# Gates of five chunks of an mLSTM scan on 80 partitions at once, with the first loads and row writes in another order

## The chip, the cores and the metric

The kernel runs on one core of one Trainium2 chip. The metric is the device time of one execution in microseconds (us), median of several runs. Smaller is better. In the views below PE is TensorE's matmul, PEld its weight load, DVE is VectorE, ACT is ScalarE, POOL is GpSimd, SP is SyncE, and SPq is SyncE's queue of DMA issues.

## The reference

Three layers run one after the other. The first is a gated linear attention (mLSTM) over 768 steps for 2 batches of 8 heads of 40 columns; its output, as 1536 tokens of 320 columns, goes through a routed mixture of experts (8 experts, 192 tokens each) and then through a dense mixture of 4 experts. The change touches only the first layer:

```python
for t in range(S):
    m_new = np.maximum(f_gate[:, :, t] + m, i_gate[:, :, t])
    f_stab = np.exp(f_gate[:, :, t] + m - m_new)
    i_stab = np.exp(i_gate[:, :, t] - m_new)
    m = m_new
    C = f_stab[:, :, None, None] * C + i_stab[:, :, None, None] * np.einsum('bhd,bhe->bhde', vt, kt)
    n = f_stab[:, :, None] * n + i_stab[:, :, None] * kt
    h_tilde = np.einsum('bhde,bhe->bhd', C, qt)
    nq = np.einsum('bhd,bhd->bh', n, qt)[:, :, None]
    denom = np.maximum(np.abs(nq), 1.0)
    y[:, :, t] = o * h_tilde / denom
```

## The kernel before

**Chunks and units.** The 768 steps are cut into six chunks of 128 steps. A unit is one chunk of one batch (8 heads); the loop runs over twelve units, `(c, b)` in the order (0,0), (0,1), (1,0) and so on. Inside a unit the recurrence is a masked matrix product: `scores` (L318) multiplies keys by queries, `spread` (L294 on TensorE, L301 on ScalarE) builds the matrix of decays, `weigh` (L326) multiplies the two on VectorE, `inner` (L349) multiplies the result by the values. Across chunks a state `C` is carried: `query` (L343) reads it, `outer` (L355) makes its increment from values that `weigh_v` (L309) has weighted, and `epilogue` (L358 to L406) adds both parts, normalises, and writes the token tile `xr` to `x_dram` (L405), to which a small load of `domain_probs` (L401) must have added four columns. `turn` and `logit` (L411, L420) then transpose that tile and compute its routing logits. TensorE's order within the loop's pass n is: scores of unit n+1, query and inner and outer of unit n, spread of the next unit or two, logit of unit n-2, turn of unit n-1. A spread needs both PSUM banks `db0` and `db1` (one buffer each) back from ScalarE. In pass 3 two spreads stand one behind the other, and ScalarE then opens the output gates with a sigmoid, which needs a change of its table before and after.

**Gates.** `gate(c0, c1)` computes on VectorE, for chunks c0 to c1, on 16 partitions (one for each batch and head): the running maximum `mm` by a scan along the steps (L242), the log decays (L244, L245), their running sum within the chunk `cum` (L257), a rounded copy `dhi`, and three more rows of `g3`. It is called three times: for chunk 0, chunk 1, and chunks 2 to 5, the last in two pieces around the weigh of unit (0,1). `gate_t` turns `g3` by TensorE and ScalarE into `gtr`, in which a step is a partition, and `decays` makes `dec`, the decay of a whole chunk. `rows(c)` copies the 16 rows of `dhi` for chunk c into partition 0 of one of two buffers, `MR[c % 2]`, by a DMA on SyncE's queue. The spread of chunk c reads that buffer.

**Queues.** Nearly every load is issued by SyncE in the order of the code, one behind the other: output gates (640 KB), queries and keys `qk` (416 KB for one batch of chunk 0, 832 KB for a whole chunk), keys and values `kv` (648 KB a chunk). The order is written by hand; no scheduler changes it.

## Time and profile before

| what | value |
|---|---|
| time, median of 3 runs | 651.18 us (650.54 to 651.72) |
| profiled execution, its own time | 650.6 us |
| its span, first to last instruction | 648.9 us |
| first 100 us (the scan): busy PE, DVE, ACT | 90.33, 71.70, 62.75 us |
| mean granted TensorE clock: 0 to 100, 100 to 137, after 137 us | 0.86, 0.58, 0.99 |

The scan takes about the first 100 us. The clock is told as a share of 2.4 GHz: 1.00 is the upper level and 0.50 the lower one of 1.2 GHz. A long row in a timeline may be the same work at the lower level.

### The profile page before, as it was taken

How to read it: one execution, taken by the hardware profiler on the slowest of the kernel's cores; microseconds unless marked ns; L12 is line 12 of the kernel's file. 1: busy time of each engine (PE TensorE's matmuls, PEld its weight loads, DVE VectorE, ACT ScalarE, POOL GpSimd, SP SyncE). 2: the span in 40 equal slices, each digit the busy share in tenths (PEclk: the TensorE clock that was granted, in tenths of full speed). 3: DMA queues.
4: the chain of work that ended last, by engine and by line, in shares of the span. 5: the costliest groups of instructions: out<-in, count | busy, mean ns of one | idle time of the engine just before them, and what ended most of it. 6: DMA issues, size and time to landing. Idle time of an engine off the chain costs nothing.

```text
span 648.9 us, 11110 instructions
## 1 busy us (share of the span) xinstructions
PE 604.2 (93%) x4411; PEld 529.5 (82%) x4416; DVE 296.8 (46%) x1116; ACT 182.0 (28%) x486; POOL 80.2 (12%) x126
## 2 busy tenths in 40 slices
PE   7989994588999999899999999999999999999996
PEld 3879992277887778797898989898989898989885
DVE  8744887877787666303242232322234231313221
ACT  8648720012222225422221113221123211111120
POOL 6000000201220124300110001200011000002022
PEclk9867997569999999999999999999999999999998
DMA  6744415334534355901220002210000000001011
GB/s 186 233 127 120 121 51 191 105 126 147 188 105 153 118 188 203 338 11 34 66 82 0 1 1 65 67 48 0 1 2 1 0 1 1 0 1 41 0 41 41
DMA packets 13238, 52.01 MB, mean 80 GB/s; under 512 B 3499, under 2 KB 5131, under 8 KB 10491
## 3 DMA queue, kind: packets, MB, share of 16 engines
q1 hardware_dynamic: 9107, 25.10, 13.0%
q0 software_dynamic: 3904, 26.12, 11.5%
q8 instruction: 34, 0.56, 0.4%
q14 instruction: 17, 0.14, 0.1%
q10 hardware_dynamic: 176, 0.09, 0.1%
HBM read 46.91 MB, written 4.35 MB: 79 GB/s over the span
## 4 chain that ended last, share of the span: by engine, by line
PE 77%; DVE 10%; issue 6%; DMA 3%; POOL 2%; ACT 1%; POOLq 0%; SPq 0%; DVEq 0%
PE y L1187 8%; PE y L1189 8%; PE y L1188 8%; PE z L1175 7%; PE z L1177 6%; PE z L1176 6%; PE y L929 5%; PE px L349 4%; PE z L916 4%; PE z L1179 3%; PE z L1180 3%; PE pr L645 3%; PE st L318 2%; DVE cmp L598 2%; PE px L343 1%
## 5 line engine op out<-in xcount | busy, mean ns | idle before, releaser
L1227 DVE SCALAR_TENSOR_TENSOR h2l<-z,h2h 128x512 fp32r<-128x512 f32 x96 | 66.4, 692 | 240.5 <-ACT h2h L1226 239.4
L1226 ACT ACTIVATE h2h<-z 128x512 fp32r<-128x512 f32 x96 | 57.4, 598 | 263.9 <-PE z L1180 259.6
L1189 PE MATMUL y<-wh,h2l 128*128 128x320 f32 x384 | 118.6, 309 | 0.0
L1187 PE MATMUL y<-wh,h2h 128*128 128x320 f32 x384 | 118.4, 308 | 0.0
L1188 PE MATMUL y<-wl,h2h 128*128 128x320 f32 x384 | 118.1, 308 | 0.0
L1175 PE MATMUL z<-X2h,wh 128*128 128x512 f32 x192 | 76.7, 399 | 0.8 <-DVE X2l L964 0.8
L1187 PEld LDWEIGHTS y<-wh,h2h 128*128 128x128 f32 x384 | 72.1, 188 | 4.5
L1177 PE MATMUL z<-X2h,wl 128*128 128x512 f32 x192 | 75.7, 394 | 0.0
L1176 PE MATMUL z<-X2l,wh 128*128 128x512 f32 x192 | 75.3, 392 | 0.0
L1188 PEld LDWEIGHTS y<-wl,h2h 128*128 128x128 f32 x384 | 72.1, 188 | 4.0
L1189 PEld LDWEIGHTS y<-wh,h2l 128*128 128x128 f32 x384 | 72.0, 188 | 0.0
L929 PE MATMUL y<-h,w 128*128 128x192 f32 x256 | 55.7, 338 | 0.0
L916 PE MATMUL z<-xt,w 128*128 128x192 f32 x256 | 55.6, 338 | 0.0
L569 POOL TENSOR_TENSOR wl<-raw,wh 128x512 fp32r<-128x512 f32 x16 | 20.6, 1288 | 204.1 <-ACT wh L562 204.1
L916 PEld LDWEIGHTS z<-xt,w 128*128 128x128 f32 x256 | 42.0, 192 | 4.2 <-issue 3.8
L1177 PEld LDWEIGHTS z<-X2h,wl 128*128 128x128 f32 x192 | 36.0, 188 | 9.4
L929 PEld LDWEIGHTS y<-h,w 128*128 128x128 f32 x256 | 41.5, 190 | 2.6 <-issue 1.5
L645 PEld LDWEIGHTS <-oh 128*128 128x128 bf16 x504 | 21.0, 98 | 25.4 <-issue 15.5
L1175 PEld LDWEIGHTS z<-X2h,wh 128*128 128x128 f32 x192 | 36.0, 188 | 5.5 <-DVE X2l L964 1.1
L919 ACT ACTIVATE h<-z 128x192 f32<-128x192 f32 x64 | 21.2, 331 | 66.3 <-PE z L916 62.4
L1176 PEld LDWEIGHTS z<-X2l,wh 128*128 128x128 f32 x192 | 36.0, 188 | 4.5
L1179 PE MATMUL z<-X2h,wh 128*128 128x512 f32 x96 | 38.3, 399 | 0.0
(241 smaller groups left out, 860.1 us busy)
## 6 DMA issues: line engine op xcount, KB each, us to landing
raw<-in_m2w_dram SPq DMA_DIRECT2D x20, 512.0 KB, 3.7
qk<-in_qk_dram SPq DMA_DIRECT2D x5, 832.0 KB
kv<-in_kv_dram SPq DMA_DIRECT2D x6, 648.0 KB, 11.4
x_dram<-xr SPq DMA_DIRECT2D x12, 194.0 KB, 2.0
sig<-in_og_dram SPq DMA_DIRECT2D x1, 1280.0 KB
raw<-in_m2w_dram SPq DMA_DIRECT2D x4, 256.0 KB, 7.2
qk<-in_qk_dram SPq DMA_DIRECT2D x2, 416.0 KB
sig<-in_og_dram SPq DMA_DIRECT2D x1, 640.0 KB
```

The source lines that it names most:

```text
L645: T.matmul(pc[:, :NC], oh[:, c], cmp[:, c], start=(c == 0), stop=(c == NT - 1))
L916: T.matmul(Z[f], w1[:, k * F + f * P:k * F + (f + 1) * P], xt[:, k], start=False, stop=(k == 1), skip_group_check=True)
L929: T.matmul(Y[0][:, i * CAP:(i + 1) * CAP], w2[:, f * DM + i * P:f * DM + (i + 1) * P], h, start=(f == 0 and i == 0), stop=(f == NF - 1), s ...
L1175: T.matmul(z, hi[:, c], xh[:, k], start=(k == 0), stop=False)
L1176: T.matmul(z, hi[:, c], xl[:, k], start=False, stop=False)
L1177: T.matmul(z, lo[:, c], xh[:, k], start=False, stop=False)
L1179: T.matmul(z, hi[:, c], xh[:, 2], start=False, stop=False)
L1187: T.matmul(y[:, :DM], hh[:, ts], hi[:, c], start=(f == 0), stop=False)
L1188: T.matmul(y[:, :DM], hh[:, ts], lo[:, d], start=False, stop=False)
L1189: T.matmul(y[:, :DM], hl[:, ts], hi[:, c], start=False, stop=(f == NF - 1))
L1226: A.activation(hh, z, AF.Relu)
L1227: V.scalar_tensor_tensor(hl, z, 0.0, hh.bitcast(F32), op0=OP.max, op1=OP.subtract)
```

## The change

Chunk 0 is computed as before, on 16 partitions, with one edit in the order. Then one scan over 640 steps gives the running maximum of chunks 1 to 5. Two DMAs (`spread_max`) copy that maximum, once shifted by a step, from 16 partitions of 640 to 80 partitions of 128 (`mx`), where a partition is one chunk of one head. The raw gates come to the same 80 partitions as a second copy of the input (`fx` and `ix`, 40 KB each, loaded on ScalarE's queue at the start). `gates_rest` does the remaining eight operations once for 80 partitions, and one multiplication for the chunk decays in place of four. `gates_rest_t` transposes four blocks of 80 columns, and ScalarE evicts them in three instructions.

The order changes with it. The second batch of chunk 0 (`load(0, 1)`) is loaded ahead of `kv` of chunk 0; `qk` of chunk 1 is loaded ahead of the decay rows of chunk 1; the decay rows of chunks 1 and 2 are written one behind the other ahead of `kv` of chunk 1, and those of chunks 3, 4 and 5 in passes 1, 3 and 4 in place of 2, 4 and 5. The gates' transposes stand in pass 0 in place of before the loop and pass 1. In the diff, lines that are only taken out of `gate`, `gate_t` and `decays` are not repeated.

```diff
+            X = NCH - 1
+            XB = X * BH
+            g3 = big.tile([112, P], F32, name="g3")
+            dl, io, cum = (big.tile([BH, P], F32, name=n) for n in ("dl", "io", "cum"))
+            dhi = big.tile([BH, P], F32R, name="dhi")
+            fx, ix, dlx, cumx, rst = (big.tile([XB, P], F32, name=n) for n in ("fx", "ix", "dlx", "cumx", "rst"))
+            dhx = big.tile([XB, P], F32R, name="dhx")
+            mx = big.tile([XB, 2, P], F32, name="mx")
+            g4 = big.tile([XB, 3, P], F32, name="g4")
+            for t, r0 in ((fx, 0), (ix, BH)):
+                nc.scalar.dma_start(t, gatex[r0 // BH])
             pat = big.tile([P, P], F32, name="pat")
             step = big.tile([P, P], F32R, name="step")
             MR = [big.tile([P, BH, P], F32R, name=f"mr{i}") for i in range(2)]
-            sel = [big.tile([BH, P], F32, name=f"sel{r}") for r in range(2)]
-            own = [big.tile([BH, 2 * HB], F32, name=f"own{r}") for r in range(2)]
-            de = [big.tile([BH, NCH, 2 * HB], F32, name=f"de{r}") for r in range(2)]
+            sel = [big.tile([XB, P], F32, name=f"sel{r}") for r in range(2)]
+            own = big.tile([XB, X, BH], F32, name="own")
+            de = big.tile([XB, X, B, 2, HB], F32, name="de")
             dec = big.tile([P, NCH, 2 * HB], F32, name="dec")
             gtr = big.tile([P, 4, NCH, BH], F32, name="gtr")
             G.affine_select(MR[1], zero[:, :, None].to_broadcast([P, BH, P]), pattern=[[0, BH], [1, P]],
                             compare_op=OP.not_equal, fill=-BIG, base=1, channel_multiplier=-1)
             A.activation(own2, own2, AF.Sigmoid)
-            V.memset(rst.rearrange("p (c t) -> p c t", t=P)[:, :, 0:1], 0.0)
             V.memset(g3, 0.0)
+            G.affine_select(own, zero[:XB, :, None].to_broadcast([XB, X, BH]), pattern=[[-1, X], [-X, BH]],
+                            compare_op=OP.not_equal, fill=1.0, base=0, channel_multiplier=1)
...
-                nc.sync.dma_start(MR[c % 2][0:1].bitcast(F32), dhi[:, c * P:(c + 1) * P].bitcast(F32))
+                src = dhx.rearrange("(h c) t -> c h t", c=X)[c - 1] if c else dhi
+                nc.sync.dma_start(MR[c % 2][0:1].bitcast(F32), src.bitcast(F32))
+
+            ft, it = gt[0:BH], gt[32:32 + BH]
+
+            def scan_max(c0, c1):
                 s = slice(c0 * P, c1 * P)
+                V.tensor_tensor_scan(mm[:, c0 * P + 1:c1 * P + 1], ft[:, s], it[:, s], mm[:, c0 * P:c0 * P + 1],
+                                     op0=OP.add, op1=OP.max)
+
+            def gate(f, i, m0, m1, dl, cum, dhi, io, g, ge, gl, n):
+                V.tensor_add(dl, f, m0)
+                V.tensor_sub(dl, dl, m1)
+                if n == BH:
                     V.memset(dl[:, 0:1], 0.0)
+                V.tensor_tensor_scan(cum, rst[:n], dl, 0.0, op0=OP.mult, op1=OP.add)
+                V.tensor_scalar(dhi, cum, 0.0, None, op0=OP.add)
+                V.tensor_sub(io, i, m1)
+                V.tensor_sub(g, io, cum)
+                V.tensor_scalar(ge, g, cum[:, P - 1:P], None, op0=OP.add)
+                V.tensor_sub(gl, dhi.bitcast(F32), cum)
+
+            def gates_first():
+                p = bank("lg", bufs=2)
+                T.transpose(p[:, :112], g3, ident[:112, :112])
+                for k, f in enumerate((AF.Copy, AF.Exp, AF.Exp, AF.Exp)):
+                    A.activation(gtr[:, k, 0], p[:, 32 * k:32 * k + BH], f)
+
+            def spread_max():
+                for i in range(2):
+                    nc.sync.dma_start(mx[:, i], mm[:, P + i:S + i])
+
+            def gates_rest():
+                gate(fx, ix, mx[:, 0], mx[:, 1], dlx, cumx, dhx, dlx, g4[:, 0], g4[:, 1], g4[:, 2], XB)
+                V.tensor_scalar(de.rearrange("p c b r j -> p c (b r j)"), own, cumx[:, P - 1:P], None, op0=OP.mult)
+
+            def gates_rest_t():
+                p = bank("lg", bufs=2)
+                for k, x in enumerate((g4[:, 0], g4[:, 1], dhx.bitcast(F32), g4[:, 2])):
+                    T.transpose(p[:, XB * k:XB * k + XB], x, ident[:XB, :XB])
+                d = p[:, 4 * XB:4 * XB + 8 * X]
                 for r in range(2):
+                    T.matmul(d, sel[r], de[:, :, :, r], start=(r == 0), stop=(r == 1))
+                q = p[:, :4 * XB].rearrange("p (k h c) -> p k c h", k=4, h=BH)
+                A.activation(gtr[:, 0, 1:], q[:, 0], AF.Copy)
+                A.activation(gtr[:, 1:, 1:], q[:, 1:], AF.Exp)
+                A.activation(dec[:, 1:], d.rearrange("p (c h) -> p c h", h=8), AF.Exp)
 
...
-            for f in gate(0, 1):
-                f()
+            scan_max(0, 1)
+            gate(ft[:, :P], it[:, :P], mm[:, :P], mm[:, 1:P + 1], dl, cum, dhi, io, g3[0:BH], g3[32:32 + BH],
+                 g3[96:96 + BH], BH)
+            V.tensor_scalar(g3[64:64 + BH], dhi.bitcast(F32), 0.0, None, op0=OP.add)
+            rows(0)
+            load(0, 1)
             load_kv(0)
+            scan_max(1, NCH)
+            spread_max()
+            load(1)
             A.activation(own2, own2, AF.Exp)
-            gate_t(0, 1)
+            gates_first()
             spread(*units[0])
             scores(*units[0])
             warm(CR['W1'])
-            weigh_v(*units[0])
-            for f in gate(1, 2):
-                f()
-            load(0, 1)
-            load(1)
-            load_kv(1)
             V.memset(ohs[0][:, 0:1], 0.0)
             weigh(*units[0])
-            gates = gate(2, NCH)
-            for f in gates[:5]:
-                f()
             spread(*units[1])
+            weigh_v(*units[0])
+            gates_rest()
+            rows(1)
+            rows(2)
+            load_kv(1)
             nc.scalar.dma_start(wg, wgate)
             load_o(CR['SO'], NCH)
-            gate_t(1, 2)
-            decays(1, 2)
             for n, (c, b) in enumerate(units):
                 if b == 0:
                     if c + 2 < NCH:
                     query(c, b)
                 if n < last:
                     weigh(*units[n + 1])
-                if n == 0:
-                    for f in gates[5:]:
-                        f()
                 if n < 2:
                     warm(CR['W3'][n])
                 inner(c, b)
                     outer(c, b)
                 if n < last:
                     weigh_v(*units[n + 1])
-                if n == 1:
-                    gate_t(2, NCH)
-                    decays(2, NCH)
-                if n == 2:
-                    rows(3)
-                if n == 4:
-                    rows(4)
-                if n == 5:
-                    rows(5)
+                if n == 0:
+                    gates_rest_t()
                 while len(GG) < min(last + 1, n + 3 + (n >= 3)):
                     spread(*units[len(GG)])
-                if n == 1:
-                    rows(2)
+                if n in (1, 3, 4):
+                    rows({1: 3, 3: 4, 4: 5}[n])
...
+    gatex = gates.reshape(2, BH, NCH, P)[:, :, 1:].reshape(2, (NCH - 1) * BH, P)
```

SyncE's queue, from the decay rows of chunk 0 on. `mr_138` and `mr_139` are the two buffers of decay rows before, `mr_147` and `mr_148` the same two after the change; `xr` and `x_dram` belong to the first unit's epilogue. Before:

```order
L229 DMA mr_138<-dhi 1x16x128
L184 DMA kv<-in_kv_dram 128x1296
L229 DMA mr_139<-dhi 1x16x128
L180 DMA qk<-in_qk_dram 104x1024
L180 DMA qk<-in_qk_dram 104x2048
L184 DMA kv<-in_kv_dram 128x1296
L187 DMA sig<-in_og_dram 128x2560
L180 DMA qk<-in_qk_dram 104x2048
L184 DMA kv<-in_kv_dram 128x1296
L401 DMA xr<-in_dprob_dram 128x4
L405 DMA x_dram<-xr 128x388
L229 DMA mr_138<-dhi 1x16x128
```

With the change:

```order
L231 DMA mr_147<-dhi 1x16x128
L180 DMA qk<-in_qk_dram 104x1024
L184 DMA kv<-in_kv_dram 128x1296
L260 DMA mx<-mm 80x1x128 x2
L180 DMA qk<-in_qk_dram 104x2048
L231 DMA mr_148<-dhx 1x16x128
L231 DMA mr_147<-dhx 1x16x128
L184 DMA kv<-in_kv_dram 128x1296
L187 DMA sig<-in_og_dram 128x2560
L180 DMA qk<-in_qk_dram 104x2048
L184 DMA kv<-in_kv_dram 128x1296
```

The decay rows of chunk 2, the last row of the first list, have moved from behind the first write of `x_dram` to a place ahead of `kv` of chunk 1. The two copies of the maximum stand between `kv` of chunk 0 and `qk` of chunk 1.

VectorE, around the weigh (`pm`) of the first two units. Before, from the weigh of unit (0,0) on:

```order
L326 TENSOR_TENSOR pm_268<-st0_226,gg_217 128x512
L326 TENSOR_TENSOR pm_268<-st1_227,gg_217 128x512
L242 SCALAR_TENSOR_TENSOR mm_119<-gt_66,mm_119 16x512
L244 TENSOR_TENSOR dl_131<-gt_66,mm_119 16x512
L245 TENSOR_TENSOR dl_131<-dl_131,mm_119 16x512
L257 SCALAR_TENSOR_TENSOR cum_133<-rst_134,dl_131 16x512
L250 TENSOR_SCALAR dhi_135<-cum_133 16x512
L326 TENSOR_TENSOR pm_315<-st0_305,gg_280 128x512
L326 TENSOR_TENSOR pm_315<-st1_306,gg_280 128x512
L255 TENSOR_SCALAR g3_130<-dhi_135 16x512
L259 TENSOR_TENSOR io_132<-gt_66,mm_119 16x512
```

With the change, from the weigh of unit (0,0) to that of unit (0,1):

```order
L316 TENSOR_TENSOR pm_250<-st0_235,gg_226 128x512
L316 TENSOR_TENSOR pm_250<-st1_236,gg_226 128x512
L241 TENSOR_TENSOR dlx_137<-fx_135,mx_141 80x128
L242 TENSOR_TENSOR dlx_137<-dlx_137,mx_141 80x128
L245 SCALAR_TENSOR_TENSOR cumx_138<-rst_139,dlx_137 80x128
L246 TENSOR_SCALAR dhx_140<-cumx_138 80x128
L247 TENSOR_TENSOR dlx_137<-ix_136,mx_141 80x128
L248 TENSOR_TENSOR g4_142<-dlx_137,cumx_138 80x128
L249 TENSOR_SCALAR g4_142<-g4_142,cumx_138 80x128
L250 TENSOR_TENSOR g4_142<-dhx_140,cumx_138 80x128
L264 TENSOR_SCALAR de_152<-own_151,cumx_138 80x80
L316 TENSOR_TENSOR pm_304<-st0_294,gg_257 128x512
```

The gates of chunk 1, which stood ahead of the first of these rows, and those of chunks 2 to 5 are now one block of nine between the two weighs, and that block reads `mx`.

TensorE, from the outer product to the spread (`db`). Before, in pass 1:

```order
L355 MATMUL py_168<-wv_344,kv_204 40x41 x8
L276 MATMUL lg_449<-ident_69,g3_130 128x112 x4
L285 MATMUL lg_458<-de0_144,sel0_140 128x32
L285 MATMUL lg_458<-de1_145,sel1_141 128x32
L294 MATMUL db0_462<-mr1_139,step_137 128x512
L294 MATMUL db1_464<-mr1_139,step_137 128x512
```

With the change, in pass 0:

```order
L345 MATMUL py_171<-wv_266,kv_208 40x41 x8
L269 MATMUL lg_335<-ident_69,g4_142 128x80 x2
L269 MATMUL lg_335<-ident_69,dhx_140 128x80
L269 MATMUL lg_335<-ident_69,g4_142 128x80
L272 MATMUL lg_335<-de_152,sel0_149 128x40
L272 MATMUL lg_335<-de_152,sel1_150 128x40
L284 MATMUL db0_345<-mr1_148,step_146 128x512
L284 MATMUL db1_347<-mr1_148,step_146 128x512
```

The transposes of the gates and the products for the chunk decays have moved one pass earlier, ahead of the spread of unit (1,0).

## Rows read from the trace of the kernel before

**Rows 1.** The page's first line: the span of the profiled execution.
```profile
span 648.9 us, 11110 instructions
```

**Rows 2.** Stretches: us, busy PE, PEld, DVE, ACT, POOL (instructions), clock, DMA share, GB/s.
```profile
0.00:10.00 10.00, 8.28 (x34) 3.48 (x35) 8.11 (x31) 7.76 (x16) 6.11 (x31) 1.00 0.61 180
10.00:15.00 5.00, 2.27 (x12) 1.39 (x12) 4.79 (x12) 4.80 (x24) 3.85 (x3) 0.89 0.73 181
15.00:20.00 5.00, 4.78 (x29) 4.41 (x30) 4.69 (x7) 2.00 (x12) 0.78 (x5) 0.50 1.02 269
20.00:30.00 10.00, 9.95 (x120) 8.64 (x121) 8.27 (x25) 7.48 (x33) 0.00 (x0) 0.97 0.84 264
35.00:44.00 9.00, 9.00 (x62) 8.51 (x62) 1.63 (x5) 4.18 (x17) 0.00 (x0) 0.50 0.74 192
44.00:48.00 4.00, 2.46 (x24) 1.59 (x24) 3.13 (x12) 2.87 (x12) 0.00 (x0) 0.93 0.16 50
48.00:58.00 10.00, 10.00 (x74) 9.34 (x73) 2.85 (x9) 8.56 (x19) 0.00 (x0) 0.50 0.34 84
```

**Rows 3.** Pieces of the chain that ended last: start us, length us, what.
```profile
9.91 4.66 DMA qk<-in_qk_dram
...
31.81 2.11 DMA mr<-dhi
...
35.01 1.17 PE lg L420 x6
...
44.66 0.44 PE db L294
...
45.13 2.19 ACT gg L301 x8
...
47.86 0.94 PE lg L420 x6
...
57.28 1.12 PE db L294 x2
...
70.14 0.61 PE lg L420 x6
...
75.35 0.66 PE db L294 x2
```

**Rows 4.** TensorE's timeline: start us, length us, line, tiles, count, idle before.
```profile
8.06 0.70 PE L294 MATMUL db<-mr,step 128*128 128x512 f32 x2 [0.23 <-DMA mr<-dhi]
...
14.71 2.08 PE L318 MATMUL st<-qk 40*128 40x128 f32 x16 [2.71 <-DMA qk<-in_qk_dram]
...
21.29 0.73 PE L294 MATMUL db<-mr,step 128*128 128x512 f32 x2
...
25.73 0.60 PE L276 MATMUL lg<-ident,g 112*128 112x112 f32 x4
...
26.82 0.73 PE L294 MATMUL db<-mr,step 128*128 128x512 f32 x2
```

**Rows 5.** VectorE's timeline, from the gates of the second chunk on.
```profile
7.49 0.47 DVE L242 TENSOR_TENSOR_SCAN mm<-gt,mm 16x128 f32<-16x128 f32 x1
7.99 0.28 DVE L244 TENSOR_TENSOR dl<-gt,mm 16x128 f32<-16x128 f32 x1
...
8.62 0.41 DVE L257 TENSOR_TENSOR_SCAN cum<-rst,dl 16x128 f32<-16x128 f32 x1
9.07 0.21 DVE L250 TENSOR_SCALAR dhi<-cum 16x128 fp32r<-16x128 f32 x1
...
12.26 1.27 DVE L242 TENSOR_TENSOR_SCAN mm<-gt,mm 16x512 f32<-16x512 f32 x1
```

**Rows 6.** SyncE's queue: issues around the first write of a token tile.
```profile
13.04 1.10 SPq L401 DMA_DIRECT2D xr<-in_dprob_dram  x1
31.38 0.33 SPq L405 DMA_DIRECT2D x_dram<-xr  x1
```

**Rows 7.** ScalarE's timeline: the eight weighted values of one unit.
```profile
15.09 1.91 ACT L309 ACTIVATE wv<-kv,gtr 128x41 f32<-128x41 f32 x8
```

More of the change, by code (lines that the diff above doesn't have):

```diff
@@ L46, in tile_mlstm_moe_moe @@
 @with_exitstack
-def tile_mlstm_moe_moe(ctx: ExitStack, tc: tile.TileContext, gates, qk, kv, og, wgate, dprob,
+def tile_mlstm_moe_moe(ctx: ExitStack, tc: tile.TileContext, gates, gatex, qk, kv, og, wgate, dprob,
                        m1w1, m1w2, m2w, out, dbg=None):
@@ L193, in attention @@
             load(0, 0)
-            g3 = big.tile([112, S], F32, name="g3")
-            dl = big.tile([BH, S], F32, name="dl")
-            io = big.tile([BH, S], F32, name="io")
-            cum = big.tile([BH, S], F32, name="cum")
-            rst = big.tile([BH, S], F32, name="rst")
-            dhi = big.tile([BH, S], F32R, name="dhi")
+            X = NCH - 1
[9 more added lines that the diff above has]
+                nc.scalar.dma_start(t, gatex[r0 // BH])
             pat = big.tile([P, P], F32, name="pat")
@@ L211, in attention @@
             V.memset(rst, 1.0)
-            V.memset(rst.rearrange("p (c t) -> p c t", t=P)[:, :, 0:1], 0.0)
             V.memset(g3, 0.0)
+            G.affine_select(own, zero[:XB, :, None].to_broadcast([XB, X, BH]), pattern=[[-1, X], [-X, BH]],
+                            compare_op=OP.not_equal, fill=1.0, base=0, channel_multiplier=1)
             for r in range(2):
-                G.memset(own[r], 1.0)
-                for s_, b_ in ((1, 0), (-1, 0)):
-                    G.affine_select(own[r].rearrange("p (b j) -> p b j", j=HB), own[r].rearrange("p (b j) -> p b j", j=HB),
-                                    pattern=[[-H * s_, B], [-s_, HB]], compare_op=OP.is_ge, fill=0.0,
-                                    base=b_ - HB * r * s_, channel_multiplier=s_)
                 G.memset(sel[r], 0.0)
@@ L270, in gate_t @@
-            def gate_t(c0, c1):
-                n = c1 - c0
-                for i0 in range(0, n, 4):
-                    m = min(4, n - i0)
-                    p = bank("lg", bufs=2)
-                    for i in range(m):
-                        T.transpose(p[:, 112 * i:112 * i + 112], g3[:, (c0 + i0 + i) * P:(c0 + i0 + i + 1) * P],
-                                    ident[:112, :112])
-                    p3 = p[:, :112 * m].rearrange("p (i h) -> p i h", h=112)
-                    for k, f in enumerate((AF.Copy, AF.Exp, AF.Exp, AF.Exp)):
-                        A.activation(gtr[:, k, c0 + i0:c0 + i0 + m], p3[:, :, 32 * k:32 * k + BH], f)
@@ L282, in decays @@
-            def decays(c0, c1):
-                p = bank("lg", bufs=2)[:, :8 * (c1 - c0)]
-                for r in range(2):
-                    T.matmul(p, sel[r], de[r][:, c0:c1], start=(r == 0), stop=(r == 1))
-                A.activation(dec[:, c0:c1], p.rearrange("p (c h) -> p c h", h=8), AF.Exp)
+                V.tensor_tensor_scan(mm[:, c0 * P + 1:c1 * P + 1], ft[:, s], it[:, s], mm[:, c0 * P:c0 * P + 1],
[4 more added lines that the diff above has]
+                if n == BH:
+                    V.memset(dl[:, 0:1], 0.0)
+                V.tensor_tensor_scan(cum, rst[:n], dl, 0.0, op0=OP.mult, op1=OP.add)
[4 more added lines that the diff above has]
+                V.tensor_sub(gl, dhi.bitcast(F32), cum)
@@ L1284, in _layout @@
     m1w1 = np.concatenate([a1[:, :P], a1[:, P:2 * P], third], -1).reshape(E1 * P, -1)
-    arrays = dict(gates=gates, qk=qk, kv=kv, og=og, wgate=wg, dprob=dp, m1w1=m1w1, m1w2=w2(inputs["moe_w2"]), m2w=m2w)
+    gatex = gates.reshape(2, BH, NCH, P)[:, :, 1:].reshape(2, (NCH - 1) * BH, P)
+    arrays = dict(gates=gates, gatex=gatex, qk=qk, kv=kv, og=og, wgate=wg, dprob=dp, m1w1=m1w1, m1w2=w2(inputs["moe_w2"]), m2w=m2w)
     return {n: np.ascontiguousarray(a) for n, a in arrays.items()}
```

31 lines of the change are left out of this document (removed).

## Prediction, written before the changed kernel ran

> **What bounds the kernel now.** I read the page first, then the windows, the chain of work that ended last, and the timelines of the engines of the first 100 us. The profiled execution took 650.6 us, 1.7 more than its span [rows 1]; the median of the runs shown is 651.2, so 0.6 is added to what the trace gives. The change ends with the scan, so the scan's end is what counts: everything behind it waits for its logits, and I take it to move with them.
>
> The scan has one regular pace. From the logits of one pass to the spread of that pass the chain goes through TensorE alone, and a pass takes 75.35 - 70.14 = 5.21 us plus 0.66 for the spread, 5.87 in all [rows 3]. The first 58 us miss that pace in five places.
> - TensorE waits 2.71 us for `qk` of the second batch [rows 4], a load issued at 9.91 that lands 4.66 us later [rows 3].
> - It then works from 15 to 20 us at a clock of 0.50 [rows 2].
> - At 31.81 it waits 2.11 us for the decay rows of chunk 2 [rows 3]. Their issue stands in SyncE's queue behind the first `x_dram` write, which goes out only at 31.38 because the small `xr` load issued at 13.04 lies behind 4 MB of loads [rows 6].
> - After that wait the clock is 0.50 from 35 to 44 us [rows 2]: logits to end of spread, 35.01 to 44.66, take 9.65 us in place of 5.21 [rows 3].
> - In pass 3 the second spread waits for ScalarE (2.19 us in the chain at 45.13). TensorE is busy for 2.46 of the 4 us around it, and from 48 to 58 us the clock is 0.50 again [rows 2]: 47.86 to 57.28 take 9.42 us [rows 3].
>
> So each pause of some 1.5 to 2.7 us costs its length and then about four more.
>
> **The change, part by part.** *VectorE's work.* The call for chunk 1 and that for chunks 2 to 5 take 12 operations each, of 0.2 to 0.5 us and of 0.4 to 1.3 us [rows 5]. In their place stand one scan over 640 steps, estimated from 0.47 us at 128 and 1.27 at 512 [rows 5] as 1.54, and nine operations on 80 x 128. No row shows 80 partitions; the nearest are the same operations on 16 x 128. VectorE's duration might grow with the rows (five times as long, 14 us for the nine) or not at all (2.7 us with gaps); the weigh in the same place has 128 partitions and the page gives no sign of such growth, so I take 2.7. The saving itself is worth nothing: TensorE waits for loads while these operations run.
>
> *The maximum's round trip* is a new wait. The scan of chunk 1 began at 7.49 [rows 5]; with two memsets cut from 768 to 128 columns ahead of it I take 6.9 for the long one, which then ends near 8.4. The two `mx` copies are issued at 8.4 to 9.4. The least they can take is what a small row copy takes on an empty queue, 2.11 us [rows 3], so 10.5. But by the shapes 2.43 MB of loads stand up to and with them: gates 96 KB, `fx` and `ix` 80, output gates 640, `qk` twice 416, `kv` 648, `mx` 80. At 180 GB/s to 10 us and 181 from there [rows 2] these are through at 13.5. The trace's 4.66 us for 416 KB behind a `kv` load speaks for the late end, which I take: 13.5 (10.5 to 15).
>
> VectorE stands still from the first weigh (done at 11.8) to 13.5, with weigh (0,1) queued behind. TensorE needs that weigh only for the inner product of pass 1, at about 20, so the wait is covered by 3 us; beyond that it goes on the path. `dhx` is the fourth operation: 0.28 + 0.28 + 0.41 + 0.21 with gaps, 14.8 [rows 5]. The row copy of chunk 1 then takes at least 2.11 us (16.9) and lies behind `qk` of chunk 1, 0.85 MB: 0.27 MB by 15 us at 181 GB/s, the rest at 269 [rows 2], through at 17.2. Spread (1,0) can start at 17.5 (16.9 to 19.2, the latter if `mx` lands at 15).
>
> *TensorE up to there.* The first spread starts at 8.06 [rows 4]; `fx` and `ix` in front of ScalarE's table load and among the loads cost perhaps 0.3. ScalarE's two first units of decays end near 13.4 (2.19 us each), the weighted values of unit (0,0) at 15.3 [rows 3, 7]. With its `qk` loaded first, scores (0,1) waits only for the weigh, at 11.9 in place of 14.71; inner at 13.5 when `kv` is there, outer done by 15.9, the gates' transposes when the block of nine ends, 16.4 to 17. So spread (1,0) waits for the rows, at 17.5 in place of 21.29 [rows 4]: **-3.8** (-4.4 to -2.1).
>
> *Moved transposes.* Pass 1 loses the stretch from 25.73 to 26.82 [rows 4], **-1.1**; in pass 0 they lie in the time that was costed above.
>
> *Decay rows of chunk 2.* Issued at about 15.5, they land near 17.6, and pass 2 reaches them ten us later. The wait from 31.81 to the spread goes: **-2.2** [rows 3]. With it goes what followed, 9.65 - 5.21 [rows 3]: **-4.4**, and 0.3 in the slower spread.
>
> *Pass 3.* The wait for ScalarE stays: two spreads, one pair of banks. Whether the clock falls after it is open. Before, the fall left 9.42 - 5.21 = **-4.2** to be had and 1.12 - 0.66 = 0.5 in the spread [rows 3].
>
> *What is late next.* By the same rates `qk` of chunk 2 lands at 27 to 29 and TensorE asks for it near 29: **+0.8** (0 to 2). ScalarE's sigmoid between two table loads, so far hidden by slow matmuls, comes to the path: **+0.7** (0 to 1.5). The decay rows of chunk 3 follow the first `x_dram` write as before, so they land about 33, and are asked for near 35.
>
> The sum: -3.8 - 1.1 - 2.2 - 4.7 - 4.7 + 0.8 + 0.7 = -15.0, so 635.6 of the profiled execution and about 636 as a median.
>
> **The rivals.** A is this sum, with a clock at the upper level from 11 us on: 636 (633.5 to 638).
>
> B: one pause still lowers the clock. For it speaks pass 3, whose wait is unchanged and which before sufficed by itself: 2.46 of 4 us busy, then 0.50 [rows 2]. Against it, the same pause can fall otherwise relative to the clock's changes. Or it is pass 0, where TensorE now rests some 1 to 2 us before spread (1,0). Either gives back 4.2 to 4.7: 640.5 (638 to 642). The Trainium skill ("TensorE: Matmul & The Clock Gate", section "A second HAM failure mode: psum-queue depth-cycling") says that short idle times between groups of matmuls can make the clock go down and up again and again. The 44 to 48 us row agrees; by that rule alone the forecast would be B or C rather than A.
>
> C: both pauses do. 636 + 9 = 645 (642 to 647).
>
> D: the freed time is given back to loads. The loads of chunks 1 and 2 end near 31 us before as after, and a TensorE that is ready earlier waits for them. Against: the loads keep ahead by the rates above. For it, if they run at 181 GB/s to 30 us in place of 264 [rows 2], `qk` of chunk 2 is 6 us late, and the pause lowers the clock: about 650.
>
> E, the other side: the round trip of the maximum is late. All five chunks hang on it. Spread (1,0) is 4.0 us behind `mx`, so at 17.3 the head gains nothing, and every us beyond costs one; with a pause of over 3 us in pass 0 the clock falls (+4.5). The other gains without pass 3 are 1.1 + 2.2 + 4.7 = 8.0, so it decides from `mx` at about 21. If it lands at 23: 655. Only a queue that holds small copies behind loads issued later would do that; no row shows one.
>
> **How the numbers follow.** A 0.40, B 0.32, C 0.12, D 0.08, E 0.08. The likeliest is 636. The range of 633.5 to 646.5 holds A, B and most of C. This kernel's runs can tell a change of about 0.2%, 1.3 us. Faster 0.87 (A to C and part of D), same 0.04 (the rest of D), slower 0.09 (E and late mishaps).
>
> **What would show it.** Right: scores (0,1) near 12; `mx` landed by 14; spread (1,0) at 17 to 18; no wait of TensorE for `mr` in pass 2; clock 1.00 in the windows from 15 to 30 and the scan's end some 14 us earlier. Wrong: a `dlx` that waits past 16; a clock of 0.50 anywhere from 18 to 45; a TensorE that waits for `qk` or `mr` after 25 us; or time behind the scan that grows.

## The result, and the profile after

| | before | with the change |
|---|---|---|
| median of 4 runs each, us | 651.45 (650.54 to 656.51) | 643.60 (638.04 to 645.05) |
| profiled execution, us | 650.6, span 648.9 | 642.28, span 640.6 |
| first `flag` of the routing on VectorE (end of the scan), us | 105.03 | 95.49 |

The ratio is 0.985, with a 95% interval of [0.980, 0.990]: the change makes the kernel faster, and 643.6 lies in the range of 633.5 to 646.5, but between rival B (640.5) and rival C (645), not at the 636 of rival A. The four runs lie 7 us apart. The three runs of before that were known lay within 1.2 us, but the fourth, 656.51, lies 6 us above the lowest: the kernel before scatters nearly as far. Ratios, here and below, are worked out from the single runs, without two slow ones (654.1 of rows2_late, 658.88 of before_fill), and need not be those of the medians.

The first reading is the windows of the page of the change, with the same columns as [rows 2]: us, busy time of PE, PEld, DVE, ACT, POOL (instructions), granted clock, DMA share, GB/s.

```profile
span 640.6 us, 11077 instructions
...
0.00:10.00 10.00, 7.67 (x31) 3.21 (x33) 7.42 (x24) 7.18 (x14) 6.24 (x27) 1.00 0.66 177
10.00:15.00 5.00, 4.84 (x32) 3.32 (x32) 2.58 (x7) 4.09 (x17) 3.57 (x7) 0.66 0.95 253
15.00:20.00 5.00, 4.24 (x54) 3.69 (x55) 4.43 (x15) 4.30 (x21) 0.00 (x0) 1.00 0.81 241
20.00:30.00 10.00, 9.95 (x123) 8.94 (x122) 7.28 (x24) 8.86 (x38) 0.00 (x0) 1.00 0.89 265
30.00:37.00 7.00, 5.47 (x68) 4.58 (x67) 5.44 (x18) 5.56 (x24) 0.00 (x0) 1.00 0.43 113
37.00:48.00 11.00, 11.00 (x80) 10.19 (x79) 3.56 (x13) 9.64 (x23) 0.00 (x0) 0.53 0.55 149
48.00:58.00 10.00, 10.00 (x127) 9.38 (x127) 8.04 (x28) 7.45 (x31) 0.00 (x0) 1.00 0.62 166
```

Of the stretches at 0.50 in [rows 2], those from 15 to 20 us and from 35 to 44 are gone, and the one behind pass 3, from 48 to 58, has only moved, to 37 to 48. One new, short one stands from 10 to 15 us. TensorE's timeline (start, length, line, tiles, count, idle before and its releaser) says where it still waits.

```profile
8.54 0.70 PE L284 MATMUL db<-mr,step 128*128 128x512 f32 x2 [1.05 <-DMA mr<-dhi]
...
12.51 1.71 PE L308 MATMUL st<-qk 40*128 40x128 f32 x16
...
18.51 0.70 PE L284 MATMUL db<-mr,step 128*128 128x512 f32 x2 [0.77 <-DMA mr<-dhx]
...
28.17 0.73 PE L284 MATMUL db<-mr,step 128*128 128x512 f32 x2
...
35.76 0.50 PE L284 MATMUL db<-mr,step 128*128 128x512 f32 x1 [1.00 <-ACT gg L291]
36.79 0.51 PE L284 MATMUL db<-mr,step 128*128 128x512 f32 x1 [0.54 <-ACT gg L291]
```

Against [rows 4]: the scores of unit (0,1) start at 12.51 without a wait (14.71 before, after 2.71 us), the spread of unit (1,0) at 18.51 (21.29), the first spread of chunk 2 at 28.17 without a wait (before, the copy's 2.11 us stand in the chain [rows 3], and TensorE itself waited 1.91 of them). Left are the two pauses of pass 3, for ScalarE. The chain of work that ended last (start, length, what) shows the price of these:

```profile
9.39 4.28 DMA mx<-mm
13.66 0.29 DVE dlx L241
...
15.08 3.29 DMA mr<-dhx
18.51 0.70 PE db L284 x2
...
34.56 2.18 ACT gg L291 x8
36.79 0.51 PE db L284
37.30 0.80 PE lg L410 x6
...
46.57 1.15 PE db L284 x2
47.72 0.72 PE lg L410 x6
...
53.04 0.66 PE db L284 x2
```

From the logits at 37.30 to the spread at 46.57 are 9.27 us, where the pace is 5.21; one pass later, from 47.72 to 53.04, it is 5.32. VectorE's timeline has the new operations:

```profile
7.15 1.54 DVE L237 TENSOR_TENSOR_SCAN mm<-gt,mm 16x640 f32<-16x640 f32 x1
...
13.66 0.29 DVE L241 TENSOR_TENSOR dlx<-fx,mx 80x128 f32<-80x128 f32 x1 [1.66 <-DMA mx<-mm]
...
14.79 0.22 DVE L246 TENSOR_SCALAR dhx<-cumx 80x128 fp32r<-80x128 f32 x1
...
16.15 1.28 DVE L316 TENSOR_TENSOR pm<-st,gg 128x512 f32<-128x512 f32 x2
```

The scan of 640 steps took 1.54 us, as estimated, and an addition on 80 x 128 takes what one on 16 x 128 took, 0.29 against 0.28 [rows 5].

**Where the time came from.** Each step from one unit's first spread to the next can be read from the `db` rows of TensorE's timeline (starts; the units are in the order of the passes). The last three columns are the profiles of after_again (the change once more), fill03 (the change with the pauses of passes 0 and 3 filled) and order_fill (the old gates in the new order, filled), described below:

| us | before | change | change again | filled (0 and 3) | old gates, filled |
|---|---|---|---|---|---|
| spread (1,0) starts | 21.29 | 18.51 | 18.45 | 18.02 | 18.17 |
| to (1,1) | 5.53 | 4.40 | 6.01 | 4.41 | 7.15 |
| to (2,0) | 7.24 | 5.26 | 5.25 | 5.25 | 5.58 |
| to (2,1) | 10.53 | 5.86 | 5.86 | 5.87 | 5.87 |
| to (3,1), over pass 3 | 12.62 | 12.47 | 8.40 | 8.41 | 8.40 |
| to (4,0) | 6.33 | 6.47 | 5.88 | 5.87 | 5.87 |
| spread (4,0) starts | 63.54 | 52.97 | 49.85 | 47.83 | 51.04 |
| first `flag` | 105.03 | 95.49 | 91.33 | 89.96 | 93.58 |

From before to the change: 2.78 in the head, 1.13 for the moved transposes, 1.98 + 4.67 for the decay rows of chunk 2 and the low clock behind them, 0.15 in pass 3, less 0.14: 10.57 us. In the scan's tail 1.03 of them are lost, where the clock is 0.60 from 88 to 92 us in the change and 1.00 from 88 to 105 before, so 9.54 are left at the first `flag`. Behind it the change takes 545.1 us to the end of the span and before 543.9.

### The profile page after: what moved, and what is told of

It is laid out like the page before. It is cut to its first block, busy times and chain, and to the rows that moved or that the text cites. A ratio compares the mean times of both kernels' runs of the same rounds, so it can differ in the third digit from the quotient of the medians.

```text
span 640.6 us, 11077 instructions
## 1 busy us (share of the span) xinstructions
PE 599.1 (94%) x4406; PEld 524.3 (82%) x4411; DVE 289.4 (45%) x1101; ACT 180.9 (28%) x479; POOL 79.4 (12%) x121
## 4 chain that ended last, share of the span: by engine, by line
PE 78%; DVE 11%; issue 5%; DMA 2%; POOL 1%; ACT 1%; POOLq 0%; SPq 0%; DVEq 0%
PE y L1170 8%; PE y L1168 8%; PE y L1169 8%; PE z L1156 7%; PE z L1158 6%; PE z L1157 6%; PE y L910 5%; PE z L897 4%; PE px L339 4%; PE z L1160 3%; PE z L1161 3%; PE pr L626 3%; DVE cmp L579 2%; PE st L308 2%; PE px L333 1%
```

## The experiments

Twelve kernels in three sets; each set has its own chip and its own runs of the kernel before (650.72, 646.80 and 647.49 us in the median). `busy(n)` stands for n matmuls into columns of a PSUM bank that nothing reads; a pause is called filled where such matmuls were put into it. The cuts of code are against the kernel before or against the change, as the text says; `...` marks lines left out.

| | median, us (runs) | ratio to before on that chip | first `flag` in its profile |
|---|---|---|---|
| 1 order_only | 646.71 (11) | 0.9938 [0.9907, 0.9968] | 100.26 |
| 1 rows2_early | 648.37 (11) | 0.9941 [0.9911, 0.9972] | 101.67 |
| 1 rows2_late | 647.33 (5) | 0.9896 [0.9836, 0.9955] | 107.90 |
| 1 fill3 | 639.98 (5) | 0.9813 [0.9760, 0.9866] | 93.01 |
| 2 order_all | 637.92 (4) | 0.9868 [0.9853, 0.9883] | 96.39 |
| 2 before_fill | 648.30 (11) | 1.0029 [0.9997, 1.0060] | 110.33 |
| 2 fill03 | 634.00 (5) | 0.9836 [0.9806, 0.9865] | 89.96 |
| 2 fx_late_fill03 | 634.08 (5) | 0.9809 [0.9796, 0.9823] | 90.07 |
| 3 after_again (the change) | 635.44 (6) | 0.9820 [0.9800, 0.9840] | 91.33 |
| 3 order_again | 638.33 (6) | 0.9856 [0.9828, 0.9884] | 96.60 |
| 3 rows3_late | 642.09 (6) | 0.9923 [0.9905, 0.9942] | 102.08 |
| 3 order_fill | 636.65 (5) | 0.9832 [0.9810, 0.9854] | 93.58 |

My theory after the result: the order of loads and row copies makes the gain, the gates on 80 partitions carry little of it, and the missing part is the clock behind pass 3. The rivals: the gates are what counts; and, the clock is a symptom that costs nothing by itself.

**order_only**: the old gates, with `qk` of the second batch ahead and the rows of chunk 2 issued ahead of the loop, nothing else.

```diff
+            load(0, 1)
             load_kv(0)
...
-            load(0, 1)
             load(1)
...
             spread(*units[1])
+            rows(2)
...
-                if n == 1:
-                    rows(2)
```

> The old gates on 16 partitions, with only two edits of order: the second batch's qk loaded ahead of kv of chunk 0, and the decay rows of chunk 2 issued before the loop. Theory 1 (the gain comes from two pauses of TensorE that go, and from the low clock after them): scores of unit (0,1) near 12 us, no wait for the rows of chunk 2; VectorE's longer gates hold the first two totals back until 22 us, so some 2.5 us later than the change: about 646 us (642 to 649) against 651 before. Theory 2 (the gain is VectorE's 7 us of gates): within 1.5 us of the kernel before, 650 or more.

646.71 us: about 0.6%, where the change has 1.5%. Two waits took the place of the two removed. ScalarE stood in its weighted values, waiting for `kv`, with the gates behind it, and TensorE waited for these; and the rows of chunk 3, one pass further, were late:

```profile
17.66 1.01 PE L226 MATMUL lg<-wup 128*128 128x512 bf16 x2 [4.24 <-ACT gtr L280]
41.89 1.19 PE L294 MATMUL db<-mr,step 128*128 128x512 f32 x2 [2.45 <-DMA mr<-dhi]
```

So two of the change's moves alone don't make its gain, and the rest had to be looked for in its other moves.

**rows2_early**: the kernel before with one edit, the rows of chunk 2 ahead of the load of the output gates.

```diff
             spread(*units[1])
+            rows(2)
             nc.scalar.dma_start(wg, wgate)
             load_o(CR['SO'], NCH)
...
-                if n == 1:
-                    rows(2)
```

> The kernel before with one edit: the decay rows of chunk 2 are issued before the loop, ahead of the output gates, and not behind the first write of a token tile. Theory 1: the 2.1 us wait in pass 2 goes and with it the low clock from 35 to 44 us: 2.2 + 4.7 less, about 644.5 us (643 to 647). Theory 2 (VectorE's work): no change beyond 1.3 us.

648.37 us, 2.35 below before, where 6.9 were expected. The wait for chunk 2 went; in its place TensorE waits 4.74 us for the rows of chunk 3, which stand in SyncE's queue right behind the loads of a chunk. Chain and TensorE:

```profile
35.50 7.62 DMA mr<-dhi
...
43.26 1.19 PE L294 MATMUL db<-mr,step 128*128 128x512 f32 x2 [4.74 <-DMA mr<-dhi]
```

**rows2_late**: the change with this one edit undone, the rows of chunk 2 behind the first `x_dram` write.

```diff
-            rows(2)
             load_kv(1)
...
-                if n in (1, 3, 4):
-                    rows({1: 3, 3: 4, 4: 5}[n])
+                if n == 1:
+                    rows(2)
+                    rows(3)
+                if n in (3, 4):
+                    rows({3: 4, 4: 5}[n])
```

> The change with one edit undone: the decay rows of chunk 2 are issued in pass 1 again, behind the first write of a token tile. Theory 1: TensorE reaches them at 28.2 us and they land near 33, so it waits about 4.5 us, and the clock falls behind it: 4.5 to 9 us more than the change, 648 to 653 us. Theory 2: not more than 2 us more than the change, at most 645.5.

647.33 us; its interval overlaps that of the change, so the time alone settles nothing. The trace does for the place: the wait is back, 3.01 us in pass 2, with the 12.47 us of an `xr` load ahead of it in the chain. The profile is of the longest run (654.1 us; the others took 642.83 to 648.77), so nothing else is read from it.

```profile
32.29 0.72 PE L284 MATMUL db<-mr,step 128*128 128x512 f32 x2 [3.01 <-DMA mr<-dhx]
```

**fill3**: the change, with TensorE kept busy in the two pauses of pass 3.

```diff
+            def busy(n):
+                for _ in range(n):
+                    T.matmul(py[:, 2 * W:], wup[:, :P], wup[:, 2 * W:], start=True, stop=True)
...
                 for u in range(2):
+                    busy(fill[u])
...
-                    spread(*units[len(GG)])
+                    spread(*units[len(GG)], fill=(12, 6) if n == 3 and len(GG) == 6 else (0, 0))
```

> The change with 12 + 6 small matmuls put into the wait of pass 3, on a corner of a PSUM bank that nothing reads. The wait for ScalarE stays as long; TensorE is only busy in it. Theory 1: the clock stays at 1.00 behind pass 3, some 4.2 to 4.7 us less than the change's profile: about 638 us, with less scatter than 638 to 645. Rival (the clock falls for another reason, or the added matmuls delay the spread): 643 us or more, with 0.50 from 38 to 48 us as before.

639.98 us, ratio 0.981, interval [0.976, 0.987], which overlaps that of the change. Behind pass 3 the clock is 1.00 to the end of the scan, (2,1) to (3,1) takes 8.40 in place of 12.47. But in this execution the clock was 0.50 from 18.5 to 25 us, behind another pause, of 1.88 us ahead of spread (1,0).

**before_fill**: the kernel before, with its three pauses filled (34 matmuls in pass 0, 26 in pass 2, 12 and 6 in pass 3). It tells whether the clock by itself is worth anything.

```diff
+            FILL = {(2, 0): (26, 0), (3, 0): (12, 6)}
...
+                    busy(FILL.get((c, b), (0, 0))[u])
...
+                if n == 0:
+                    busy(34)
```

> The kernel before, its order untouched, with small matmuls that nothing reads in three pauses of TensorE: 34 ahead of the scores of unit (0,1), 26 ahead of the spread that waits for the rows of chunk 2, 12 + 6 in pass 3. Every wait for data stays as long. Theory 1 (behind each pause the low clock costs some 2.5 to 4.7 us more): the clock stays at 1.00 to the end of the scan, 642 us (639 to 644). Rival (the waits alone are the loss, and the low clock is covered by waits that follow): 649 to 652.

648.30 us, ratio 1.003: no gain. The clock was 1.00 from 15 to 42 us, spread (2,1) came at 40.22 in place of 44.59, and there the gain was lost: the rows of chunk 3 take 9.39 us behind the loads. The chain, and TensorE:

```profile
32.48 1.76 DMA mr<-dhi
...
36.26 9.39 DMA mr<-dhi
...
45.78 0.77 PE L301 MATMUL db<-mr,step 128*128 128x512 f32 x1 [3.87 <-DMA mr<-dhi]
```

That pause then cost a low clock from 46 to 69 us. Before, the low clock was the cover of a late copy. The 4.4 us that the prediction gave to it were there only if the copy moved too.

**order_all**: the old gates with every move of the change that they allow: also the first `weigh_v` behind the second spread, and the rows of chunks 3, 4 and 5 one pass earlier. The rows of chunk 1 stay ahead of `qk` of chunk 1, and those of chunk 2 behind `kv` of chunk 1.

```diff
-            weigh_v(*units[0])
             for f in gate(1, 2):
...
             spread(*units[1])
+            weigh_v(*units[0])
+            rows(2)
...
-                if n == 2:
-                    rows(3)
-                if n == 4:
-                    rows(4)
-                if n == 5:
-                    rows(5)
...
-                if n == 1:
-                    rows(2)
+                if n in (1, 3, 4):
+                    rows({1: 3, 3: 4, 4: 5}[n])
```

> The old gates on 16 partitions with every edit of order that they allow: the second batch's qk ahead of kv of chunk 0, the weighted values of unit (0,0) behind the spread of unit (0,1), the decay rows of chunk 2 issued before the loop and those of chunks 3, 4, 5 in passes 1, 3, 4. Theory 1: the waits for rows of chunks 2 and 3 are gone; VectorE's longer gates hold the inner product of pass 1 until 22 us (20.67 in the change) and the transposes of pass 1 stay, so about 2.5 us more than the change: 646 us (644 to 648). Theory 2 (the gates' work is the gain): 649 or more. A third reading, that the gates' work is worth nothing at all: 643 to 644.

637.92 us, ratio 0.987 [0.985, 0.988]: the order alone has most of the change's gain. Its ratio agrees best with the third of the readings, that the gates' work is worth nothing; order_again below puts it beside the change on one chip.

**fill03**: the change filled as in fill3, with 16 matmuls more ahead of spread (1,0). The cut is against fill3.

```diff
+            FILL = {(1, 0): (16, 0), (3, 0): (12, 6)}
...
-                    busy(fill[u])
+                    busy(FILL.get((c, b), (0, 0))[u])
```

> The change with small matmuls that nothing reads in two pauses: 16 ahead of the spread that waits for the rows of chunk 1 in pass 0, and 12 + 6 in pass 3. Theory 1: the low clock from 18 to 25 us, which one profile of the filled pass 3 showed, cannot come; 638 us (636.5 to 640), with a scatter of about 2 us. Rival (pass 0's pause is too short to matter): as with pass 3 filled alone, 640.

634.00 us, 12.8 below before on its chip. In the profile the clock is 1.00 in every stretch of the scan, and the first `flag` comes at 89.96. Its five runs still lie 4.8 us apart: three of 633.45 to 634.00 with a mean clock of 0.968 to 0.969, two of 637.63 and 638.22 with 0.961 and 0.959. Three of the windows:

```profile
15.00:20.00 5.00, 4.90 (x64) 4.01 (x64) 4.13 (x14) 3.79 (x18) 0.00 (x0) 1.00 0.90 282
...
30.00:37.00 7.00, 6.92 (x83) 5.86 (x81) 3.19 (x10) 5.57 (x24) 0.00 (x0) 1.00 0.53 145
37.00:48.00 11.00, 11.00 (x147) 10.22 (x147) 8.29 (x31) 10.94 (x29) 0.00 (x0) 1.00 0.43 122
```

**fx_late_fill03**: the same, with the two loads `fx` and `ix` behind the first output gates on ScalarE's queue.

```diff
-            for t, r0 in ((fx, 0), (ix, BH)):
-                nc.scalar.dma_start(t, gatex[r0 // BH])
...
             open_gate(0, CR['SO'])
+            for t, r0 in ((fx, 0), (ix, BH)):
+                nc.scalar.dma_start(t, gatex[r0 // BH])
```

> As the one before it, and the raw gates of the 80 partitions are loaded behind the first sigmoid on ScalarE's queue, not at the start. Theory: they then stand behind the first qk load and not ahead of it, so the first decay rows land 0.5 us earlier (7.9 and not 8.4) and the wait of 1.05 us ahead of the first spread is near 0.2; ScalarE's table load starts 0.85 us earlier. 0.5 us less, 637.5 us; 0 if the path runs through the copies of the maximum, which land at 13.5 either way.

634.08 us. The first spread starts at 8.06 in place of 8.45, but spread (1,0) at 18.75 in place of 18.02, since the block of nine begins at 13.76 in place of 13.18: `mx` lands later. No difference to fill03 that can be told; its ratio, 0.981 [0.980, 0.982], is the narrowest of the best.

**after_again**: the change itself, unaltered, on another chip, beside the next three.

> The change itself, unaltered, on the same chip as the next three, so that they can be compared. Ratio to the kernel before 0.985 (0.980 to 0.990), as it was measured first.

635.44 us (632.64 to 640.24), ratio 0.982 [0.980, 0.984]. The profiled execution has the pauses of pass 3 to within a hundredth, and no low clock behind them. TensorE's timeline and two windows:

```profile
37.30 0.50 PE L284 MATMUL db<-mr,step 128*128 128x512 f32 x1 [1.00 <-ACT gg L291]
38.33 0.51 PE L284 MATMUL db<-mr,step 128*128 128x512 f32 x1 [0.53 <-ACT gg L291]
...
43.97 0.73 PE L284 MATMUL db<-mr,step 128*128 128x512 f32 x2
```

```profile
20.00:24.00 4.00, 3.78 (x23) 3.38 (x22) 1.29 (x2) 3.06 (x14) 0.00 (x0) 0.60 1.05 355
...
38.00:48.00 10.00, 9.67 (x121) 8.94 (x122) 6.15 (x21) 9.94 (x25) 0.00 (x0) 1.00 0.59 157
```

Logits at 38.67, spread at 43.97: 5.30 where the first profile has 9.27. Its low stretch is another one, 0.60 from 20 to 24 us, behind a wait of 1.63 ahead of spread (1,0); it costs 1.6 us, 6.01 from (1,0) to (1,1) in place of 4.40. The same program takes one of B's two ways in one execution, the clock falling behind pass 3, and the other, behind the pause of pass 0, in another. A clock at the upper level through the whole scan, as A has it, was seen only with the pauses filled.

**order_again**: order_all once more, on the same chip as the change. What lies between the two is VectorE's work, the round trip of `mx`, the place of the transposes, and the two places in SyncE's queue named above.

> The old gates with every edit of order, unaltered, beside the change. If the gates on 80 partitions are worth nothing, the two medians agree within 1.3 us. If VectorE's shorter work and the moved transposes count, this is later by the 1.9 us by which its spread of unit (1,0) was later in the profiles (20.43 against 18.51), up to 3.4 us (that of unit (1,1), 26.32 against 22.91).

638.33 us against 635.44: 2.9 us of the 12.05 that the change gains on this chip, but the intervals, [0.983, 0.988] and [0.980, 0.984], overlap by a little. In its profile the clock fell after pass 3 ((2,1) to (3,1) in 11.58 us), in that of the change it did not.

**rows3_late**: the change with one edit undone, the rows of chunk 3 back in pass 2, behind the loads.

```diff
+                if n == 2:
+                    rows(3)
...
-                if n in (1, 3, 4):
-                    rows({1: 3, 3: 4, 4: 5}[n])
+                if n in (3, 4):
+                    rows({3: 4, 4: 5}[n])
```

> The change with one edit undone: the decay rows of chunk 3 are issued in pass 2, behind the loads of chunk 3, and not in pass 1. If the row copies' places in the queue are what counts, they land near 42 us and TensorE asks for them at 36: 5 to 6 us of wait in place of the 1.5 us for ScalarE, and the clock falls behind it for longer: 4 to 9 us more than the change. If that edit is worth nothing, as the forecast had it, within 1.3 us of the change.

642.09 us, 6.65 more than the change on this chip, and the intervals are far apart. SyncE's queue has the two loads and then the copy, the chain 7.67 us for that copy, and TensorE waits 5.94 us:

```profile
34.86 0.35 SPq L180 DMA_DIRECT2D qk<-in_qk_dram  x1
35.31 0.33 SPq L184 DMA_DIRECT2D kv<-in_kv_dram  x1
35.73 0.52 SPq L231 DMA_DIRECT2D mr<-dhx  x1
...
43.53 1.19 PE L284 MATMUL db<-mr,step 128*128 128x512 f32 x2 [5.94 <-DMA mr<-dhx]
```

Then the clock is 0.53 from 41 to 50 us and 0.50 from 50 to 55. Undoing this edit, which the prediction costed at nothing, takes back 6.65 of the 12.05 us that the change gains on this chip.

**order_fill**: order_all with 24 matmuls in pass 0 and 12 and 6 in pass 3, so that old and new gates are compared at the same clock.

> The old gates with every edit of order, and small matmuls that nothing reads in two pauses: 24 in the wait of pass 0 for ScalarE, 12 + 6 in pass 3. If pauses and the clock behind them are the whole story, about what the change with filled pauses has (ratio 0.981 to 0.984); if the gates on 80 partitions count, 1.9 to 3.4 us more than that, 0.985 to 0.988.

636.65 us, ratio 0.983 [0.981, 0.985], the same as fill03 by ratio; each on its own chip. By the times this is the reading in which pauses and clock are the whole story. The traces show a difference all the same. They have both a clock of 1.00 between spreads (1,0) and (1,1), and there they differ, by 2.74 us (last two columns of the table above): with the old gates TensorE waits for VectorE, which holds `tot` behind its gates, and has the transposes still to do.

```profile
21.88 1.98 PE L356 MATMUL px<-kv,pm 128*128 128x123 f32 x16 [1.57 <-DVE tot L391]
...
24.23 0.60 PE L276 MATMUL lg<-ident,g 112*128 112x112 f32 x4
24.76 0.63 PE L285 MATMUL lg<-de,sel 16*128 16x32 f32 x4
25.32 0.73 PE L301 MATMUL db<-mr,step 128*128 128x512 f32 x2
```

At spread (4,0) it is 3.2 us (51.04 against 47.83). At the first `flag` it is 3.6 (93.58 against 89.96), but there the clocks differ too: order_fill has 0.66 from 86 to 90 us. The total times show nothing of it that their intervals allow to be told.

## Why the prediction was right, and where not

**Head (-3.8): right in kind, measured -2.78.** `mx` landed at 13.67 (13.5 predicted, from the bytes that lay ahead), `dhx` was done at 15.01 (14.8). The row copy of chunk 1 took 3.29 us; 2.4 were allowed for it. The first spread came 0.48 later than before (0.3 was said). So spread (1,0) at 18.51 lies in the bounds of 16.9 to 19.2, a microsecond behind the value taken.

**Moved transposes (-1.1): right**, -1.13, and VectorE's operations on 80 partitions cost what was taken. Rival E's late maximum did not come.

**What was to be seen.** `mx` by 14, no wait for `mr` in pass 2 and a clock of 1.00 from 15 to 30 us came; the scores of (0,1) were 0.5 late, spread (1,0) 0.5 beyond its 17 to 18. A clock of 0.50 between 18 and 45, named as a sign of error, came with the fall behind pass 3 (0.53 from 37 to 48 us), the scan's end came 9.5 us earlier in place of 14, and the time behind the scan grew by 1.2 us. Two of the prediction's readings were off without changing its sum: 44.66 in [rows 3] is the start of a spread, not its end, and the 2.11 us at 31.81 are the copy's. Its 1.3 us for what runs can tell came from three runs; the interval of the result is over 3 us wide on either side.

**Decay rows of chunk 2 (-2.2, and -4.4 - 0.3 for the clock): right as a sum** (-1.98 and -4.67), **wrong in its cause**. It was put down to one edit. Alone, that edit gave 2.35 us of the whole kernel's time (rows2_early), since the rows of chunk 3 were then late, and the clock held up alone gave nothing (before_fill). The step that failed is the sentence on the rows of chunk 3, which prices their new place at nothing. That they are in time in the change was right: issued at 30.90, they hold up no spread, and at 35.76 TensorE waits for ScalarE alone. But "as before" was not: before, they were issued at 35.96, behind the loads, and asked for only at 46.33, behind the late rows of chunk 2 and the slow matmuls. SyncE and TensorE before, and SyncE in the change:

```profile
35.96 0.51 SPq L229 DMA_DIRECT2D mr<-dhi  x1
...
46.33 0.49 PE L294 MATMUL db<-mr,step 128*128 128x512 f32 x1 [1.00 <-ACT gg L301]
47.36 0.50 PE L294 MATMUL db<-mr,step 128*128 128x512 f32 x1 [0.54 <-ACT gg L301]
```

```profile
30.90 0.52 SPq L231 DMA_DIRECT2D mr<-dhx  x1
```

Left in their old place they are late as soon as chunk 2 is not, and that costs 6.65 us (rows3_late). With the right question, what is late next once chunk 2 is not, this edit would have been seen as a large part of the gain.

**Clock after pass 3 (-4.2 - 0.5): open, as said, and decided against A in the profile of the result.** 12.62 became 12.47 there, where A needed 12.62 - 4.2 = 8.4; the fall at 48 us moved to 37. With the slower spread (6.47 against 5.88) that is 4.7 us, the difference between the 10.57 us of the scan and some 15. With the pauses of pass 3 as they are, the clock fell behind them in four profiles (before, the change, order_all, order_again) and held in one (after_again, 8.40). With the pauses filled it held in four of four (8.40 to 8.42; before_fill, which waits there for a late copy, is left aside). So the pause most likely lowers the clock, but the same pause does not always; nine profiles are few, and by total time the filled change cannot be told from the change (ratios 0.981 and 0.984 against 0.985 and 0.982, with intervals that overlap). The Trainium skill ("TensorE: Matmul & The Clock Gate", section "A second HAM failure mode: psum-queue depth-cycling") says that frequent short idle times between groups of matmuls made the clock of another kernel go down and up; the profile of the result agrees (0.53 from 37 to 48 us after pauses of 1.00 and 0.54), that of after_again does not (1.00 from 38 to 48 after 1.00 and 0.53). Giving A, B and C chances, with a range that holds them, was right, and it is why the measured time lies in the range. A as the likeliest was not: both profiles of the change are B, by pass 3 and by pass 0. The median fell between B and C on the first chip and at the time of A on the other, whose kernel before is 4 us faster too. A's sum itself can be read from fill03, where the clock never fell: its first `flag` comes 15.07 us earlier than before, where 15.0 were forecast. That this agrees to a tenth is luck, since the head gives 0.5 less there than forecast and the end of the scan loses 0.6, and the 1.5 taken for what is late next never came.

**"The saving itself is worth nothing"** (VectorE's work): at the old waits that holds, since TensorE waited for loads. With these gone, the old gates hold `tot` for 1.57 us (order_fill). So its worth is 1.6 us in the scan, and with the transposes some 2.7; by total times it is 2.9 on one chip with intervals that just overlap, and nothing between the filled kernels. It is seen in the trace and not settled in the time.

**`qk` of chunk 2 (+0.8) and the sigmoid (+0.7): not there.** (1,1) to (2,0) took 5.26 us without a wait. The sigmoid ran from 40.11 to 42.45 in the shadow of slow matmuls as before; in after_again, with the clock up, TensorE shows no wait from 38.67 to the spread at 43.97 either.

**"Everything behind it moves with the scan": only within some 4 us.** From the first `flag` to the end the six profiles of the result and of the first set take 542.8 to 546.7 us, the other eight 538.7 to 542.3. The two groups also differ in their chips: the kernel before takes 651.45 and 650.72 us on those of the first, 646.80 and 647.49 on those of the second. Of the 9.7 us between the two profiles of the change, 4.2 lie in the scan and 5.5 behind it, where TensorE is busy 110.2 and 114.1 of the 120 us that begin 40 us behind the `flag`. A difference of the chips could explain this, but it was not tested; only the change was profiled on both sides.

**A better version** may be the change with its pauses filled, 634.0 us (0.984 [0.981, 0.987]), with the late `fx` and `ix` 634.1 (0.981 [0.980, 0.982]). It is not shown to be one: by ratio both agree with the change itself (0.982 [0.980, 0.984] in after_again), and they did not run on the same chip. To take away the pause in pass 3 itself, the spread would need another pair of banks; that was not tried.

## What to carry to other kernels

When a wait is to be removed, ask of the next copy of the same kind whether it is in time for the faster engine; in a pipeline of chunks a low clock or one late copy can be the cover of the next. A small copy that is needed soon belongs ahead of the big loads on its queue, and the proof is to move it back alone. A pause that may or may not lower the clock belongs in the range as a spread between runs; matmuls that nothing reads, put into the pause, show in the trace what it costs. Several runs, on one chip, are needed before the time shows it.

## What the runs showed of the hardware, unexpected

- A copy of decay rows, 8 KB a chunk, takes 1.76 to 2.11 us when issued clear of loads (before_fill, before), 3.29 behind one `qk` load issued 5 us earlier (the change), and 7.62, 7.63, 7.67 and 9.39 us when issued right behind a `qk` and a `kv` load (rows2_early, order_only, rows3_late, before_fill). The Trainium skill ("DMA: Bandwidth & Descriptors", section "Queues, rings and completion order") says that the signal of a copy lands only after every earlier write of the same DMA engine; the last four agree.
- The same program with the same pauses ran at a clock of 0.53 and of 1.00 behind them. Its runs lie 7.0 us apart in the result and 7.6 on the chip of the third set. In the result the mean clock of a run goes with its time: 0.964 in the run of 638.04 us, 0.953 to 0.956 in those of 642.28 to 645.05. How much of the spread is this one pause, no run took apart; the runs of before lie 6.0 us apart in the result and up to 9.2 in the sets.
- In the change VectorE's operation for `pat` took 1.15 us, from 2.08 to 3.23, beside a selection of 2.00 us on GpSimd that began at 1.15 and ended at 3.15. Before, it ran at 3.51, after that selection, in 0.15. The memsets ahead of it had been cut, so it moved into GpSimd's time and gave back part of what they had saved: VectorE's first scan began at 3.71 in place of 4.07. The selection took 2.00 us in both kernels, so only VectorE's operation was held up; why, no run took apart. Before, and in the change:

```profile
3.51 0.15 DVE L429 TENSOR_SCALAR pat<-jp 128x128 f32<-128x128 int32 x1
```

```profile
2.08 1.15 DVE L419 TENSOR_SCALAR pat<-jp 128x128 f32<-128x128 int32 x1
```
